# Gathered rows turned later, eight weight subtractions on GpSimd, activation parts ahead of weight parts

## The chip, the core and the metric

The kernel runs on one core of a Trainium2 chip. A core has five engines that each work through a queue of their own in order: TensorE (PE: matrix products and transposes, PEld its weight loads), VectorE (DVE), ScalarE (ACT), GpSimd (POOL) and SyncE (SP, which here issues loads). Sixteen DMA engines move data. The metric is the device time of one execution in microseconds (us), lower is better.

## What is computed

Three stages follow each other. The third, in which the change lies, gives each of 1536 tokens to one of eight experts:

```
attention per (batch, head), where a query sees only keys of its own cluster -> x  (1536 x 512)
x = relu(x @ w_in)**2 @ w_out                                    # 512 -> 2048 -> 512
do = x @ w_skip > 0                                              # the other tokens pass through
e  = argmax(x[do] @ w_gate);  g = softmax(x[do] @ w_gate)[e]
out = x;  out[do] = x[do] + g * (relu(x[do] @ w1[e]) @ w2[e])    # w1: 8 x 512 x 1024, w2: 8 x 1024 x 512
```

All of it is held to float32 accuracy. A float32 product is made of three products of rounded parts: a value is split into a high part (a rounded copy) and a low part (the value minus its high part), and high x high, high x low and low x high are summed.

## The kernel before

The expert stage works in nine *units* of 128 token slots: units 0 and 1 are two blocks of the fullest expert, units 2 to 8 are the other seven experts. For a unit u the steps are these.

- `gather(u)` (L1013): GpSimd issues an indirect DMA that brings the unit's rows into a tile (`u`, or `l` for every third). Its list of rows comes from the routing: `ixA` for unit 0, `ixB` for unit 1, `ixp` for the rest. Unit 0 gathers from `out_dram`, the others from `xd`, a copy of the same rows.
- `parts(src, name)` (L1021): four transposes on TensorE into a PSUM tile `xps`, of which there are two in turn, shared with the routing's transposes at L819. Then ScalarE writes the high part (L1028: `xh` for gathered rows, `hh` for the hidden layer), and VectorE the low part (L1029: `xl`, `hl`).
- `g1(u, n)` (L1039): one half n of the hidden layer, 12 products with `wih`, `wil` into `hps`, and a Relu on ScalarE (L1043) into `hs`. `turn_h(u, n)` is `parts` of `hs`. `g2(u, n)` (L1049): 12 products with `woh`, `wol` into `acc`. `finish(u)` (L1054): VectorE scales and adds, GpSimd issues an indirect write of the rows to `out_dram`.

Expert weights are loaded by SP in pieces of 128 x 1024 into stage buffers (`st`, and `xc`, the tiles of the earlier stages). `half_weights` (L746) splits each piece: ScalarE writes the high part (L761), VectorE the low part in two subtractions of 128 x 512 (L765). The tables `ENG0`, `ENG1`, `ENG2` name the two engines for each piece of the first, the second and the later experts; each entry is `'av'` before: ScalarE and VectorE. A stage buffer is free for the next load when both have read it. The second expert's pieces are needed from unit 2 on.

Up to the beginning of unit 1 a hand-written order stands: `base()` (L1129) yields once per three products (last products of the middle stage, then unit 0), and `EVENTS` says at which count n other work is called: `'c'` a weight piece, `'l'` a step of the routing of the last 384 tokens (`late()`, L986), `'x'` `parts` of unit 0's gathered rows. A routing step `turn_x` (L812) also writes its rows to `xd` and `out_dram` from ScalarE's queue (L815, L816), transposes them (L819) and copies them out of PSUM (`xs`, L821); the logits (L825) read `xs`. Later `late()` computes ranks and a payload (`pay`, L896), sums them on TensorE (`sl`, L919), makes `ixB` and calls `gather(1)`.

`between(gen, f)` calls f after two of a generator's four groups of three products. From unit 1 on the loop at L1179 sets the order. In this stage TensorE's queue keeps the order in which the code is written (and SP's too, up to unit 1); ScalarE, VectorE and GpSimd are ordered by a scheduler that goes by priority (the order of the code) and by what it thinks is ready.

Of the kernel before, what the change touches and what calls it, by code (L numbers as in the profile page):

```python
# [7 lines left out]
F32 = mybir.dt.float32  # L8
# [4 lines left out]
ALU = mybir.AluOpType  # L13
# [23 lines left out]
PE, ACT, DVE, POOL, SP = (mybir.EngineType.PE, mybir.EngineType.Activation, mybir.EngineType.DVE,  # L37
                          mybir.EngineType.Pool, mybir.EngineType.SP)
EVENTS = ((1, 'e'), (2, 'e'), (3, 'e'), (4, 'e'), (8, 'e'), (11, 'e'), (12, 'c'), (13, 'e'), (15, 'c'),
          (16, 'cce'), (18, 'el'), (21, 'x'), (22, 'lcc'), (25, 'c'), (26, 'l'), (28, 'lc'), (30, 'l'), (34, 'll'))  # L40
ENG0 = ('av',) * 8
ENG1 = ('av',) * 8
ENG2 = ('av',) * 8
HOLD = 2
M0 = {DVE, PE, ACT, POOL}
AFTER = 0
PACE = 3
# [5 lines left out]
def clustered_attention_moe(  # L53
# [16 lines left out]
    nc = tc.nc  # L70
# [29 lines left out]
    inner = ExitStack()  # L100
    inner.enter_context(tc.manual_schedule(engines=M0))
    nc.vector.memset(slot, 1.0)
# [30 lines left out]
    def do(gen):  # L133
        for _ in gen:
            pass
# [130 lines left out]
    with ExitStack() as actx:  # L266
# [417 lines left out]
        for i in range(-LA, NQ + GT + 1):  # L684
            if i == CLOSE:
                inner.close()
            for op in ORDER.split():
                op, lag = op.rstrip("'"), op.count("'")
# [38 lines left out]
    loads = [h + (c,) for h in halves for c in (0, 2)]  # L727
    ENGS = [ENG0, ENG1] + [ENG2] * E

# [5 lines left out]
    def stage(t):  # L735
        free.append(t[:, 0:1024].rearrange("p (c f) -> p c f", c=2))
# [47 lines left out]
    def econvert_to(units):  # L784
        while edone[0] < min(units, len(halves)):
            if next(egen) == "unit":
                edone[0] += 1
# [173 lines left out]
    def early():  # L961

        for ch in range(NC - 1):
# [8 lines left out]
            if ch == NC - 2:  # L972
                pick(0, sg)
                gather(0)
            if ch < HOLD:
                stage(xc[ch])
# [9 lines left out]
    def late():  # L986
# [5 lines left out]
        gather(1)  # L992
        for ch in range(HOLD, NC):
            stage(xc[ch])
# [14 lines left out]
    UN = E + 1  # L1009
# [3 lines left out]
    def gather(u):  # L1013

        xg = xgs[u % 3]
        nc.gpsimd.memset(xg, 0.0)
        nc.gpsimd.indirect_dma_start(
            out=xg, in_=xd if u else out, in_offset=bass.IndirectOffsetOnAxis(ap=lists[u][0], axis=0),
            out_offset=None, bounds_check=N - 1, oob_is_err=False)

    def parts(src, name):  # L1021

        tps = ps_x.tile([128, 4, 128], F32, name="xps", tag="x")
        for c in range(4):
            nc.tensor.transpose(out=tps[:, c], in_=src[:, c * 128:(c + 1) * 128], identity=ident)
        hh = ep.tile([128, 4, 128], F32R, name=name + "h")
        hl = ep.tile([128, 4, 128], F32R, name=name + "l")
        nc.scalar.copy(out=hh, in_=tps)  # L1028
        nc.vector.tensor_tensor(out=hl, in0=tps, in1=hh.bitcast(F32), op=ALU.subtract)  # L1029
        return hh, hl  # L1030

    def products(ps, x, w, start, stop):
        for c in range(4):
            for i, (a, b) in enumerate(((0, 0), (0, 1), (1, 0))):
                nc.tensor.matmul(out=ps, lhsT=x[a][:, c], rhs=w[b][:, c],
                                 start=(start and c == 0 and i == 0), stop=(stop and c == 3 and i == 2))
            yield

    def g1(u, n):  # L1039
        hps = ps_h.tile([128, 512], F32, name="hps")  # L1040
        yield from products(hps, xp_t[u], hexp[max(u - 1, 0), 0, n], True, True)
        hs = ep.tile([128, 512], F32, name="hs")
        nc.scalar.activation(out=hs, in_=hps, func=AF.Relu)  # L1043
        hs_t[u, n] = hs

    def turn_h(u, n):
        hp_t[u, n] = parts(hs_t.pop((u, n)), "h")

    def g2(u, n):  # L1049
        if n == 0:  # L1050
            y_t[u] = ps_o.tile([128, DM], F32, name="acc")
        yield from products(y_t[u], hp_t.pop((u, n)), hexp[max(u - 1, 0), 1, n], n == 0, n == FB - 1)

    def finish(u):  # L1054
        yo = ep.tile([128, DM], F32, name="yo", bufs=1)
        nc.vector.scalar_tensor_tensor(out=yo, in0=y_t.pop(u), scalar=lists[u][1], in1=xgs[u % 3],
                                       op0=ALU.mult, op1=ALU.add)
        nc.gpsimd.indirect_dma_start(  # L1058
            out=out, out_offset=bass.IndirectOffsetOnAxis(ap=lists[u][0], axis=0),
            in_=yo, in_offset=None, bounds_check=N - 1, oob_is_err=False)  # L1060
# [82 lines left out]
    def between(gen, f):  # L1143
        for i, _ in enumerate(gen):
            if i == 1:
                f()
            yield

    def x_of_A():
        xp_t[0] = parts(xgs[0], "x")  # L1150
# [25 lines left out]

    econvert_to(6)
    xp_t[1] = parts(xgs[1], "x")
    for u in range(1, UN):  # L1179
        econvert_to(4 * u)  # L1180
        do(g1(u, 0))
        if u > 1:
            do(g2(u - 1, 1))
            finish(u - 1)
            turn_h(u, 0)
        if u + 2 < UN:
            gather(u + 2)
        econvert_to(4 * u + 2)
        do(g1(u, 1) if u > 1 else between(g1(u, 1), lambda: turn_h(u, 0)))
        if u + 1 < UN:  # L1190
            xp_t[u + 1] = parts(xgs[(u + 1) % 3], "x")
        do(g2(u, 0))
        turn_h(u, 1)
    do(g2(UN - 1, 1))
    finish(UN - 1)

# [65 lines left out]
```

## Time and profile before

| | |
|---|---|
| time of three runs, us | 686.8, 688.0, 688.48 (median 688.0) |
| the profiled execution, us | 688.21, of which the span is 686.5 |
| busy over the span, us | PE 655.3 (95%), DVE 481.0 (70%), ACT 415.1 (60%), POOL 253.0 (37%) |
| instructions | PE 3769, DVE 928, ACT 846, POOL 329 |

The span is what the trace covers; the time has 1.7 us around it. Times in the rows are microseconds from the span's start. The routing of the last tokens and units 0 and 1 lie between about 540 and 590, units 2 to 8 between about 586 and 678, and the last write follows. In a timeline row the bracket gives how long the engine was idle ahead of the instruction and what ended the wait. Matmul durations overlap: the spacing of starts is what counts.

### The profile page before, as it was taken

The page shows a single profiled execution, that of the slowest core. Times are in us where ns is not written, and L with a number is a line of the kernel's source. Part 1 is how long each engine was busy: PE and PEld are TensorE (multiplying, and loading weights), DVE is VectorE, ACT ScalarE, POOL GpSimd, SP SyncE. Part 2 cuts the span into 40 slices and gives each one's busy share as a digit, 9 for nine tenths or more (in the row PEclk, how much of TensorE's full clock was granted, in tenths as well). Part 3 has the DMA queues.
Part 4 walks back from the last instruction along what each step waited for, and adds up shares of the span by engine and source line. Part 5 has one row for each costly group of instructions (what it writes and reads, how often), then busy time and mean ns, then how long its engine had stood idle before and what let it go on. Part 6 is the DMA issues. An engine that isn't in the chain of part 4 may idle for free. (4 is left out here: it accounts for less than half of the span.)

```text
span 686.5 us, 11273 instructions
## 1 busy us (share of the span) xinstructions
PE 655.3 (95%) x3769; PEld 569.2 (83%) x3769; DVE 481.0 (70%) x928; ACT 415.1 (60%) x846; POOL 253.0 (37%) x329
## 2 busy tenths in 40 slices
PE   7889999999999999899999999999999898999994
PEld 6688988988888888889899999999888676888883
DVE  5678999999999999664365656522244688899950
ACT  6779989989998986444433333322232275778830
POOL 4534555536365445644344453421110203113110
PEclk9999999999999999999999999999999989999998
DMA  6567565655655200213212222101222596999900
GB/s 138 144 163 198 136 160 134 149 139 137 149 122 126 55 13 1 69 62 103 67 63 77 69 71 91 40 0 47 93 91 82 177 336 243 369 361 362 364 14 23
DMA packets 72034, 89.90 MB, mean 131 GB/s; under 512 B 32384, under 2 KB 43584, under 8 KB 71968
## 3 DMA queue, kind: packets, MB, share of 16 engines
q1 hardware_dynamic: 69664, 84.52, 41.7%
q0 software_dynamic: 1440, 3.01, 1.2%
q10 hardware_dynamic: 864, 1.57, 0.6%
q8 instruction: 32, 0.52, 0.3%
q14 instruction: 34, 0.28, 0.1%
HBM read 62.18 MB, written 9.44 MB: 104 GB/s over the span
## 5 line engine op out<-in xcount | busy, mean ns | idle before, releaser
L580 DVE TENSOR_TENSOR pl<-pt,ph 128x384 fp32r<-128x384 f32 x192 | 103.5, 550 | 19.8 <-ACT ph L571 18.3
L259 ACT ACTIVATE r<-hps 128x384 f32<-128x384 f32 x62 | 30.4, 491 | 125.8 <-PE hps L252 120.6
L557 PE MATMUL pt<-ident,p 128*128 128x128 f32 x576 | 97.1, 279 | 4.7 <-DVE pl L580 3.7
L515 PE MATMUL sc<-B,A 80*128 80x384 f32 (+1 forms) x384 | 93.4, 364 | 4.5 <-DMA A<-hi 1.8
L571 ACT CAST ph<-pt 128x384 fp32r<-128x384 f32 x192 | 89.7, 480 | 10.5 <-PE pt L557 9.7
L522 DVE TENSOR_REDUCE nm<-sc 128x1 f32<-128x768 f32 x96 | 90.9, 947 | 3.5 <-PE sc L515 3.4
L262 DVE TENSOR_TENSOR hl<-r,hh 128x384 fp32r<-128x384 f32 x62 | 37.4, 604 | 77.0 <-POOL hh L138 77.0
L531 ACT ACTIVATE p<-sc,nm 128x768 f32<-128x768 f32 x96 | 87.3, 909 | 6.0 <-DVE nm L522 5.5
L557 PEld LDWEIGHTS pt<-ident,p 128*128 128x128 f32 x576 | 70.8, 142 | 20.2 <-DVE pl L580 13.1
L138 POOL TENSOR_SCALAR hh<-r 128x384 fp32r<-128x384 f32 x62 | 36.5, 589 | 137.9 <-ACT r L260 118.8
L1087 PE MATMUL acc<-woh,hh 128*128 128x512 f32 x186 | 74.6, 401 | 0.0
L1087 PE MATMUL acc<-woh,hl 128*128 128x512 f32 x186 | 73.9, 397 | 0.0
L1087 PE MATMUL acc<-wol,hh 128*128 128x512 f32 x186 | 73.9, 397 | 0.0
L590 PE MATMUL av<-ph,vs 128*128 128x384 f32 x192 | 73.4, 382 | 0.1
L515 PEld LDWEIGHTS sc<-B,A 80*128 80x128 f32 (+1 forms) x384 | 63.9, 193 | 9.6 <-ACT p L531 5.3
L590 PE MATMUL av<-pl,vs 128*128 128x384 f32 x192 | 65.7, 342 | 0.6 <-DVE pl L580 0.6
L252 PE MATMUL hps<-A,wil 128*128 128x384 f32 x184 | 62.1, 338 | 1.8 <-POOL wil L184 1.8
L252 PE MATMUL hps<-A,wih 128*128 128x384 f32 x184 | 62.5, 340 | 0.0
L252 PE MATMUL hps<-B,wih 128*128 128x384 f32 x184 | 62.1, 337 | 0.0
L1087 PEld LDWEIGHTS acc<-woh,hl 128*128 128x128 f32 x186 | 35.3, 190 | 8.0
L1087 PEld LDWEIGHTS acc<-woh,hh 128*128 128x128 f32 x186 | 35.2, 190 | 5.8 <-DVE xc L1095 0.2
L1087 PEld LDWEIGHTS acc<-wol,hh 128*128 128x128 f32 x186 | 35.3, 190 | 5.3
(260 smaller groups left out, 1474.6 us busy)
## 6 DMA issues: line engine op xcount, KB each, us to landing
xc<-in_moe_w_dram SPq DMA_DIRECT2D x34, 512.0 KB, 5.8
st<-in_moe_w_dram SPq DMA_DIRECT2D x30, 512.0 KB, 5.7
st<-in_moe_w_in_dram SPq DMA_DIRECT2D x64, 128.0 KB, 2.9
st<-in_moe_w_out_dram SPq DMA_DIRECT2D x16, 512.0 KB, 3.5
A<-hi SPq DMA_DIRECT2D x30, 192.0 KB, 3.1
B<-hi SPq DMA_DIRECT2D x30, 192.0 KB, 3.1
qn<-in_q_dram SPq DMA_DIRECT2D x16, 192.0 KB, 3.3
kn<-in_k_dram SPq DMA_DIRECT2D x16, 192.0 KB, 3.6
```

The lines of the kernel that those rows point to most:

```text
L138: nc.gpsimd.tensor_scalar(out=o, in0=i, scalar1=1.0, scalar2=0.0, op0=ALU.mult, op1=ALU.add)
L252: nc.tensor.matmul(out=hps, lhsT=wi[w][:, c, f * 128:(f + 1) * 128], rhs=xhl[ch][a][:, c], start=(n == 0), stop=(n == 3 * KD - 1))
L259: nc.scalar.activation(out=r, in_=hps, func=AF.Relu)
L262: nc.vector.tensor_tensor(out=hl, in0=r, in1=hh.bitcast(F32), op=ALU.subtract)
L515: nc.tensor.matmul(out=sc[:, c, 0:384], lhsT=A[h][0:kk, a, t * 128:(t + 1) * 128], rhs=Bk[h][0:kk, a, c * 384:(c + 1) * 384], start=(a == ...
L522: nc.vector.tensor_reduce(out=nm_t[i], in_=sc_t[i][:, :, 0:384], op=ALU.max, axis=AX.XY, negate=True)
L531: nc.scalar.activation(out=p, in_=sc[:, :, 0:384], func=AF.Exp, bias=nm, scale=1.0, accum_out=su_t[n, c][:, t, h:h + 1])
L557: nc.tensor.transpose(out=pt[:, c], in_=p_t[i][:, n, c * 128:(c + 1) * 128], identity=ident)
L571: nc.scalar.copy(out=block(i, n)[by_pool].bitcast(F32) if by_pool else block(i, n)[0], in_=pt_t[i, n])
L580: nc.vector.tensor_tensor(out=pl, in0=pt_t.pop((i, n)), in1=ph.bitcast(F32), op=ALU.subtract)
L590: nc.tensor.matmul(out=av, lhsT=vs[:, c, 2 * h:2 * h + 2].rearrange("p x d -> p (x d)"), rhs=r[:, c], start=(c == 0 and i == 0), stop=(c = ...
L1087: nc.tensor.matmul(out=acc, lhsT=h2[a][:, i * 128:(i + 1) * 128], rhs=wo[w][:, f], start=(f == 0 and n == 0), stop=(f == NF - 1 and n == 2))
```

## The change

Four edits, all in the expert stage.

1. The event `'x'` (transposes and parts of unit 0's gathered rows) moves from count 21 to count 24, so three groups of three products later.
2. `ENG1` gets `'ap'` in its first four entries: the low parts of the second expert's `w1`, eight subtractions of 128 x 512, are made by GpSimd instead of VectorE.
3. In `parts` the two part instructions are traced at a priority raised by 120, so that the scheduler may set them ahead of weight parts.
4. In the last unit the transposes of the second hidden half stand inside the products `g2(u, 0)`, after two of their four groups, instead of behind them.

```
-          (16, 'cce'), (18, 'el'), (21, 'x'), (22, 'lcc'), (25, 'c'), ...
+          (16, 'cce'), (18, 'el'), (22, 'lcc'), (24, 'x'), (25, 'c'), ...
-ENG1 = ('av',) * 8
+ENG1 = ('ap',) * 4 + ('av',) * 4
+AHEAD = 120
@@ parts
-        nc.scalar.copy(out=hh, in_=tps)
-        nc.vector.tensor_tensor(out=hl, in0=tps, in1=hh.bitcast(F32), op=ALU.subtract)
+        with tc.high_priority(offset=AHEAD):
+            nc.scalar.copy(out=hh, in_=tps)
+            nc.vector.tensor_tensor(out=hl, in0=tps, in1=hh.bitcast(F32), op=ALU.subtract)
@@ for u in range(1, UN)
-        do(g2(u, 0))
-        turn_h(u, 1)
+        if u + 1 < UN:
+            do(g2(u, 0))
+            turn_h(u, 1)
+        else:
+            do(between(g2(u, 0), lambda: turn_h(u, 1)))
```

**GpSimd, from unit 0's gather on.** `wil` is the low part of `w1`; the rows with `ixA`, `ixB` and `ixp` are the gathers of unit 0, 1 and 2. Before:

```order
L1017 DMA u<-out_dram,ixA 128x512
L1017 DMA u<-xd,ixB 128x512
L1017 DMA l_5821<-xd,ixp 128x512
L1058 DMA out_dram<-yo,ixA 1536x512
L1016 MEMSET u 128x512
```

After:

```order
L1018 DMA u<-out_dram,ixA 128x512
L766 TENSOR_TENSOR wil<-xc_91,wih 128x512 x2
L766 TENSOR_TENSOR wil<-xc_92,wih 128x512 x2
L766 TENSOR_TENSOR wil<-st,wih 128x512 x4
L1018 DMA u<-xd,ixB 128x512
L1018 DMA l_5821<-xd,ixp 128x512
L1060 DMA out_dram<-yo,ixA 1536x512
```

The eight subtractions stand between the gather of unit 0 and that of unit 1, in GpSimd's one queue.

**TensorE, around unit 0's gathered rows.** `acc` are the last products of the middle stage, `xps<-ident,u` the transposes of the gathered rows, `xps<-ident,xc_94` those of a routing block, `lps` the logits of the block before it, `hps` the first products of unit 0. Before (the row after the last one here is the first `hps`):

```order
L1025 MATMUL xps<-ident,u 128x128 x4
L1087 MATMUL acc<-woh,hh 128x512
L1087 MATMUL acc<-wol,hh 128x512
L1087 MATMUL acc<-woh,hl 128x512
L819 MATMUL xps<-ident,xc_94 128x128 x4
L825 MATMUL lps<-wgs,xs 128x9 x4
L1087 MATMUL acc<-woh,hh 128x512
L1087 MATMUL acc<-wol,hh 128x512
L1087 MATMUL acc<-woh,hl 128x512
```

After (the three products ahead of the first row have moved up):

```order
L820 MATMUL xps<-ident,xc_94 128x128 x4
L826 MATMUL lps<-wgs,xs 128x9 x4
L1089 MATMUL acc<-woh,hh 128x512
L1089 MATMUL acc<-wol,hh 128x512
L1089 MATMUL acc<-woh,hl 128x512
L1089 MATMUL acc<-woh,hh 128x512
L1089 MATMUL acc<-wol,hh 128x512
L1089 MATMUL acc<-woh,hl 128x512
L1026 MATMUL xps<-ident,u 128x128 x4
L1037 MATMUL hps<-wih,xh 128x512
L1037 MATMUL hps<-wil,xh 128x512
```

The transposes of the gathered rows stood nine products, a routing block and its logits ahead of the first `hps`; now they stand right ahead of it.

**ScalarE, at the same place.** `DMA xd` and `DMA out_dram` are a routing block's writes, `COPY xs` its copy, `CAST xh` the gathered rows' high part. Before:

```order
L815 DMA xd<-xc_94 128x512
L761 CAST wih<-st 128x1024
L816 DMA out_dram<-xc_94 128x512
L761 CAST wih<-st 128x1024
L821 COPY xs<-xps 128x512
L761 CAST wih<-st 128x1024
L1028 CAST xh<-xps 128x512
L761 CAST wih<-xc_91 128x1024
```

After:

```order
L816 DMA xd<-xc_94 128x512
L762 CAST wih<-st 128x1024
L817 DMA out_dram<-xc_94 128x512
L762 CAST wih<-st 128x1024
L822 COPY xs<-xps 128x512
L762 CAST wih<-st 128x1024
L816 DMA xd<-xc_94 128x512
L762 CAST wih<-xc_91 128x1024
L1030 CAST xh<-xps 128x512
```

Up to the first `COPY xs` the rows are the same; `CAST xh` stands one weight cast and one write later.

## Rows read from the trace of the kernel before

**Rows 1.** Stretches of 20 us: busy time (x instructions), granted clock, DMA share, GB/s.

```profile
540.00:560.00 20.00, 17.20 (x85) 13.65 (x84) 13.21 (x24) 10.08 (x13) 1.56 (x1) 0.83 0.95 333
560.00:580.00 20.00, 17.00 (x81) 12.88 (x81) 17.81 (x58) 11.46 (x15) 6.63 (x5) 0.91 0.73 243
600.00:620.00 20.00, 20.00 (x96) 16.39 (x95) 19.53 (x33) 15.47 (x21) 3.92 (x4) 1.00 1.02 362
```

**Rows 2.** Timeline of TensorE, unit 0's gathered rows: start, duration, instruction, [idle before].

```profile
548.19 0.66 PE L1025 MATMUL xps<-ident,u 128*128 128x128 f32 x4 [2.61 <-DMA u<-out_dram,ixA]
...
551.08 1.71 PE L825 MATMUL lps<-wgs,xs 128*128 128x9 f32 x8
...
553.21 0.63 PE L1087 MATMUL acc<-wol,hh 128*128 128x512 f32 x1
...
555.35 0.58 PE L1035 MATMUL hps<-wih,xh 128*128 128x512 f32 x1
```

**Rows 3.** Timeline of ScalarE: the write that waits, what stands behind it, later casts.

```profile
548.17 0.37 ACTq L816 DMA_DIRECT2D out_dram<-xc  x1
548.59 1.05 ACT L761 CAST wih<-st 128x1024 fp32r<-128x1024 f32 x1 [4.51 <-DMA u<-out_dram,ixA]
549.54 0.58 ACT L821 COPY xs<-xps 128x512 f32<-128x512 f32 x1
...
561.40 1.03 ACT L761 CAST wih<-xc 128x1024 fp32r<-128x1024 f32 x1
```

**Rows 4.** Timeline of GpSimd: the gathers of unit 0 and of unit 1.

```profile
540.58 1.56 POOL L1017 DMA_INDIRECT u<-out_dram,ixA  x1 [0.62 <-DVE hl L262]
570.09 1.38 POOL L1017 DMA_INDIRECT u<-xd,ixB  x1 [27.95 <-DMA xc<-in_moe_w_dram]
```

**Rows 5.** Instructions that write `wil`: ns min/median/max, first and last start.

```profile
L765 DVE TENSOR_TENSOR wil<-st,wih x30: 674/682/694, 544.1 to 652.0; 128x512 fp32r<-128x512 f32 x30
L184 POOL TENSOR_TENSOR wil<-u,wih x16: 1277/1390/1715, 102.1 to 436.4; 128x512 fp32r<-128x512 f32 x16
```

**Rows 6.** DMA issues from 535 to 600: queue, count, median us from issue to landing.

```profile
u<-out_dram,ixA POOLq DMA_INDIRECT x1, 7.6
u<-xd,ixB POOLq DMA_INDIRECT x1, 3.6
l<-xd,ixp POOLq DMA_INDIRECT x1, 4.8
```

**Rows 7.** Timeline of TensorE: the payload's wait, then unit 1's gathered rows.

```profile
568.03 0.24 PE L919 MATMUL sl<-pay,so 128*128 128x40 bf16 x3 [1.10 <-DVE pay L896]
...
574.62 0.60 PE L1025 MATMUL xps<-ident,u 128*128 128x128 f32 x4
575.89 0.50 PE L1035 MATMUL hps<-wih,xh 128*128 128x512 f32 x1 [0.67 <-ACT xh L1028]
...
576.82 0.50 PE L1035 MATMUL hps<-wih,xl 128*128 128x512 f32 x1 [0.20 <-DVE xl L1029]
```

**Rows 8.** Timeline of VectorE: a moved subtraction, the payload, unit 1's list.

```profile
562.96 0.69 DVE L765 TENSOR_TENSOR wil<-xc,wih 128x512 fp32r<-128x512 f32 x1
...
567.70 0.27 DVE L896 TENSOR_TENSOR pay<-oh,vals 128x120 bf16<-128x120 bf16 x1
...
569.66 0.15 DVE L929 SCALAR_TENSOR_TENSOR ixB<-sB 128x1 int32<-128x1 f32 x1
```

**Rows 9.** Timeline of the last unit: its `g2` halves and the transposes between.

```profile
670.47 0.39 PE L1035 MATMUL acc<-woh,hh 128*128 128x512 f32 x1
...
670.73 0.60 ACT L1043 ACTIVATE hs<-hps 128x512 f32<-128x512 f32 x1 [2.28 <-PE hps L1035]
...
673.27 0.60 PE L1025 MATMUL xps<-ident,hs 128*128 128x128 f32 x4
...
674.54 0.51 PE L1035 MATMUL acc<-woh,hh 128*128 128x512 f32 x1 [0.68 <-ACT hh L1028]
...
675.27 0.50 PE L1035 MATMUL acc<-woh,hl 128*128 128x512 f32 x1
```

More of the change, by code (lines that the diff above doesn't have):

```diff
@@ L39 @@
 EVENTS = ((1, 'e'), (2, 'e'), (3, 'e'), (4, 'e'), (8, 'e'), (11, 'e'), (12, 'c'), (13, 'e'), (15, 'c'),
-          (16, 'cce'), (18, 'el'), (21, 'x'), (22, 'lcc'), (25, 'c'), (26, 'l'), (28, 'lc'), (30, 'l'), (34, 'll'))
+          (16, 'cce'), (18, 'el'), (22, 'lcc'), (24, 'x'), (25, 'c'), (26, 'l'), (28, 'lc'), (30, 'l'), (34, 'll'))
 ENG0 = ('av',) * 8
-ENG1 = ('av',) * 8
+ENG1 = ('ap',) * 4 + ('av',) * 4
 ENG2 = ('av',) * 8
 HOLD = 2
+AHEAD = 120
 M0 = {DVE, PE, ACT, POOL}
```

## The prediction

> **What bounds the kernel now.** I read the busy time by stretches first, then TensorE's timeline where it is not full, then the queues of whoever it waits for. [...]
>
> At unit 0's gathered rows it idles 2.61 us, and ScalarE is stuck at the same point: its write to `out_dram` (548.17) goes only when the gather, which reads `out_dram`, has landed (540.58 + 7.6 = 548.2), and behind that write stand a cast and the copy `xs`, done at 549.54 + 0.58 = 550.12 [rows 2 to 4, 6]. Around the routing of the last tokens it waits 1.10 us for the payload, then 0.67 and 0.20 us for unit 1's parts [rows 7]. In the last unit it waits 0.68 us for `hh`, and a little more for `hl` [rows 9].
>
> [...] Products start every 0.233 us at the upper level (12 in 2.80 us) [rows 9] and every 0.43 us at the lower (553.21 to 555.35, five products) [rows 2].
>
> **Edit 1, gathered rows three groups later.** TensorE goes on where it stood: three products (0.7 us) and a routing block's transposes (0.6 us), from 545.6 to 546.9. Next in its queue are the logits, which need `xs`. In ScalarE's order nothing ahead of that copy has moved, so it still ends at 550.12. The idle spell is then about 3.2 us instead of 2.6 us. The logits start at about 550.1 instead of 551.08, a gain of 1.0 us; owed are the gathered rows' transposes (0.4 us at the upper level, 0.9 us at the lower). And those now stand right ahead of the first `hps`, so that `xh` and `xl`, hidden before by some 6 us of other work, are waited for. The same sequence exists for unit 1: 0.67 + 0.20 us of waiting [rows 7]. Sum: -1.0 + 0.4 to 0.9 + 0.9, so 0.3 to 0.8 us later, and I take 0.6. [...]
>
> **Edit 2, eight subtractions to GpSimd.** What it removes: VectorE's eight subtractions of 0.68 us [rows 5], of which the first stands at 562.96, inside the chain of small routing operations that ends in the payload at 567.70 [rows 8]. Four of the eight lie ahead of the payload, 2.4 us and more; TensorE's wait of 1.10 us for it goes, even with unit 0 shifted by 0.6. [...] TensorE is then ready for unit 1's gathered rows not at 574.62 but at 574.62 + 0.6 - 1.1 = 574.1, or 572.3 if the clock stays up.
>
> What it adds: GpSimd takes 1.28 to 1.72 us for this shape, median 1.39 [rows 5], and the order of after puts all eight between the gathers of unit 0 and unit 1, in one queue. The first can start when ScalarE's cast of the first piece of that expert is done: 561.40 + 1.03 = 562.4 before [rows 3], 563.2 with the shift of edit 1 and its knock-on on ScalarE. Eight of them take 10.2 us (minimum) to 11.1 us (median), so the queue is free at 573.4 to 574.3; I take 573.9. The gather of unit 1 went out at 570.09 before, as soon as its list was ready at 569.66 + 0.15 [rows 4, 8]. Now the list waits for the queue, and the gather leaves 3.8 us later.
>
> It has little slack to pay this from. It took 3.6 us to land (573.7), 0.9 us ahead of the transposes that read it [rows 6, 7]. For a gather that leaves at 573.9 the nearest row is the next one, 4.8 us, issued as weight loads picked up again; the ends are 3.6 and, among busy loads, 7.6 us [rows 6]. So it lands at 578.7, with 577.0 and 581.5 as ends. Behind this wait on TensorE stands all the rest, since unit 1's first products need those rows. Against 574.62 that is **+4.1 us** (+2.4 to +6.9). Edit 1's shift and the saved payload wait are both swallowed by it.
>
> [...] By the two rows of the clock this costs 1.8 to 3.4 us [rows 1]; the first part of it passes in the wait for `xh` and `xl`, so I take the lower end, **+1.8 us**.
>
> VectorE still makes the low parts of `w2` pieces at this time, from two inputs in SBUF. The median and the maximum of GpSimd's row differ by 0.33 us [rows 5], which eight times is 2.7 us. [...] I stay with the median, since it was taken with VectorE at work too (70% of the span).
>
> **Edit 3, parts ahead of weights.** In units 2 to 8 there is no wait of TensorE to remove [rows 1], so nothing is gained. The price is that ScalarE and VectorE now stand at a part that waits for TensorE while a weight piece could be done. Cover: VectorE's last `wil` starts at 652.0 [rows 5], while the last unit's first half of `hps` begins 36 products ahead of 670.47 [rows 9], at about 662, so pieces are some 9 us early. I cost it at zero; without that cover it would be up to one part, 0.6 to 0.7 us, per unit.
>
> **Edit 4, last transposes inside products.** `hs` is ready at 670.73 + 0.60 = 671.3; six products after 670.47 is 671.9, so the transposes need not wait. The two parts then pass under the other six products. The wait of 0.68 us goes, and of 675.27 - 674.54 = 0.73 us between the first and third product 0.47 remains: 0.68 + 0.27 = 0.95, so **-1.0 us**. Nothing later covers this; it counts in full.
>
> **Sum.** +4.1 + 1.8 - 1.0 = +4.9 us. The profiled execution took 688.21 us, 0.2 us more than the median of 688.0, so I add the sum to the median: 692.9 us. With the ends of the gather and of the clock: +2.4 + 0 - 1.0 = +1.4 gives 689.4, +6.9 + 3.4 - 1.0 = +9.3 gives 697.3.
>
> **Rivals.** *The cast comes early.* If the clock holds at unit 0, ScalarE's cast of the second expert's first piece comes some 2 us earlier (560.4), the queue is free at 571.5, and the gather, with still idle DMA engines, lands at 575.1. That is +0.5 for the gather, -1.0 for the tail, 0 to +1.8 for the clock: 687.5 to 689.3, no change. [...]
>
> *Faster: the relief of VectorE decides.* If the queue on GpSimd let the gather go by about 568.7, it would land when TensorE is ready at 572.3. Then the payload's 1.1 us, the second fall of the clock, 1.8 us, and the tail's 1.0 us are won, less the 0.6 of edit 1: 684.7. It takes eight subtractions in some 5.5 us, 0.69 us each, VectorE's own pace; GpSimd's shortest row is 1.28 us. It decides from the point where GpSimd is done before unit 1's list is.
>
> *Much slower: contention and loads.* With 1.72 us each [rows 5] the queue is free at 576.9, the loads run again, the gather takes 7.6 us [rows 6] and lands at 584.5: +9.9 + 3.4 - 1.0 = +12.3, 700.3 us.
>
> **How the numbers follow.** A measurement of this kernel can tell about 0.3% (2.1 us) from no change. Forecast 0.60 (in 689.4 to 697.3, of which the lowest 0.02 lies within 0.3%), the early cast 0.21, the faster rival 0.09, much slower 0.10. Faster by over 0.3%: 0.09. Within: 0.21 + 0.02 = 0.23. Slower: 0.58 + 0.10 = 0.68. The range reaches from 687.3, which takes in the early cast, to 697.3; what is left out is the faster rival and the much slower one.
>
> **What the profile of after would show.** Edit 1: idle of about 3 us ahead of the logits, released by ScalarE's `xs`, not by the gather; a wait for `xh` ahead of unit 0's first product. Edit 2: eight `wil` subtractions on GpSimd of 1.3 to 1.4 us from about 563 to 574, the gather of unit 1 right behind them, some 4 us of TensorE idle ahead of `xps<-ident,u` with that gather as releaser, and a lower clock after it; no wait for the payload. Edit 4: no wait ahead of the last `acc` products. Were the gather to leave before 571, or TensorE not to wait for it, the forecast would be wrong and the time near or below that of before.

## The result, and the profile after

The changed kernel takes 694.32 us (median of 6 runs, 693.73 to 696.52) where the kernel before took 687.95 us beside it (6 runs, 686.8 to 688.97): a ratio of 1.010, with a 95% interval of 1.0081 to 1.0119. The forecast was 692.9 us, slower, with a range of 687.3 to 697.3. The sign, the rough size and the edit that costs were forecast; the mechanism was not the one named, as the rows show.

The profiled execution took 696.52 us, with a span of 694.8 us, 8.3 us more than the one before. Line numbers are one or two higher than before. Stretches of 20 us, columns as in [rows 1]:

```profile
540.00:560.00 20.00, 15.86 (x76) 12.25 (x76) 11.50 (x25) 8.10 (x11) 2.07 (x2) 0.83 0.88 301
560.00:580.00 20.00, 13.39 (x64) 10.74 (x64) 19.46 (x53) 11.15 (x15) 11.83 (x10) 0.85 0.59 208
580.00:600.00 20.00, 19.32 (x91) 15.28 (x91) 14.67 (x24) 11.32 (x15) 4.27 (x4) 0.98 0.83 295
```

Between 560 and 580 TensorE is busy 13.39 us where it was 17.00, and VectorE, though eight subtractions lighter, 19.46 us where it was 17.81. Work was taken from VectorE and it became busier, which already speaks against the forecast. The timeline of TensorE, with the rows that answer to [rows 2, 7]:

```profile
550.95 1.88 PE L826 MATMUL lps<-wgs,xs 128*128 128x9 f32 x8 [3.47 <-ACT xs L822]
555.39 1.05 PE L1026 MATMUL xps<-ident,u 128*128 128x128 f32 x4
557.12 0.50 PE L1037 MATMUL hps<-wih,xh 128*128 128x512 f32 x1 [0.68 <-ACT xh L1030]
...
567.09 0.17 PE L874 MATMUL rk<-oh,tri 128*128 128x24 bf16 x1 [2.58 <-DVE oh L870]
...
575.91 0.24 PE L920 MATMUL sl<-pay,so 128*128 128x40 bf16 x3 [3.71 <-DVE pay L897]
...
582.37 0.60 PE L1026 MATMUL xps<-ident,u 128*128 128x128 f32 x4
```

At unit 0 the picture is the one forecast: ScalarE's write stands until the gather has landed, and `xs` behind it, as in [rows 3]:

```profile
548.95 0.37 ACTq L817 DMA_DIRECT2D out_dram<-xc  x1
549.37 1.04 ACT L762 CAST wih<-st 128x1024 fp32r<-128x1024 f32 x1 [4.55 <-DMA u<-out_dram,ixA]
...
550.32 0.58 ACT L822 COPY xs<-xps 128x512 f32<-128x512 f32 x1
```

The wait for the payload, forecast to go, has grown from 1.10 to 3.71 us, and the one ahead of the ranks (`rk`, which reads `oh`), 0.47 us in the trace of before, to 2.58 us. Ahead of unit 1's gathered rows at 582.37, where the forecast put the stall, there is no wait. GpSimd's timeline, answering to [rows 4]:

```profile
541.33 1.56 POOL L1018 DMA_INDIRECT u<-out_dram,ixA  x1 [0.62 <-DVE hl L263]
564.51 4.98 POOL L766 TENSOR_TENSOR wil<-xc,wih 128x512 fp32r<-128x512 f32 x4 [21.62 <-PE xps L1026]
569.45 5.33 POOL L766 TENSOR_TENSOR wil<-st,wih 128x512 fp32r<-128x512 f32 x4
578.13 1.40 POOL L1018 DMA_INDIRECT u<-xd,ixB  x1 [3.36 <-DVE sgp L999]
```

The eight subtractions end at 569.45 + 5.33 = 574.8, and then GpSimd sits idle for 3.36 us until unit 1's list is there: the queue waits for the list, not the list for the queue. The rows land after 3.5 us, as in [rows 6], at 581.6, ahead of the transposes at 582.37. Why the list is late, VectorE's timeline tells, answering to [rows 8]:

```profile
564.55 1.26 DVE L867 TENSOR_TENSOR oh<-oh,mr 128x24 f32<-128x24 f32 x1
565.74 0.16 DVE L889 TENSOR_REDUCE gate<-ex 128x3 f32<-128x24 f32 x1
565.85 1.19 DVE L870 TENSOR_TENSOR oh<-oh,sel 128x24 bf16<-128x24 f32 x1
566.96 1.31 DVE L890 TENSOR_SCALAR gate<-gate 128x3 f32<-128x3 f32 x1
...
568.54 0.68 DVE L1031 TENSOR_TENSOR hl<-xps,hh 128x512 fp32r<-128x512 f32 x1
...
569.43 1.33 DVE L909 TENSOR_SCALAR rkb<-rank,nA 128x3 f32<-128x3 f32 x1
570.68 1.34 DVE L895 TENSOR_TENSOR gate<-gate,vals 128x3 f32<-128x3 f32 x1
571.94 1.69 DVE L912 TENSOR_TENSOR so<-slot,rkb 128x384 bf16<-128x384 f32 x1
573.56 1.25 DVE L893 CAST vals<-gate 128x3 bf16<-128x3 f32 x1
...
575.58 0.28 DVE L897 TENSOR_TENSOR pay<-oh,vals 128x120 bf16<-128x120 bf16 x1
577.71 0.15 DVE L930 SCALAR_TENSOR_TENSOR ixB<-sB 128x1 int32<-128x1 f32 x1
```

Operations on 128 x 3 and 128 x 24 elements now last 1.19 to 1.34 us. Two of them in the kernel before:

```profile
562.57 0.18 DVE L866 TENSOR_TENSOR oh<-oh,mr 128x24 f32<-128x24 f32 x1
565.82 0.22 DVE L908 TENSOR_SCALAR rkb<-rank,nA 128x3 f32<-128x3 f32 x1
```

The instructions that write `wil` on GpSimd (ns min/median/max), answering to [rows 5], with two pieces of four subtractions:

```profile
L766 POOL TENSOR_TENSOR wil<-xc,wih x4: 1264/1279/1291, 564.5 to 568.2; 128x512 fp32r<-128x512 f32 x4
L766 POOL TENSOR_TENSOR wil<-st,wih x4: 1269/1300/1602, 569.4 to 573.2; 128x512 fp32r<-128x512 f32 x4
```

A held operation ends with the GpSimd instruction that was running: `oh` 564.55 + 1.26 = 565.81, while GpSimd's first subtraction runs from 564.51 for some 1.26 us (to about 565.8); `rkb` ends at 570.76, GpSimd's fifth, from 569.45, at about 570.75. The seven lengthened rows shown above come to 9.4 us; before they took 1.6 us (0.18 + 0.18 + 0.16 + 0.22 + 0.16 + 0.55 + 0.16). That is 7.8 us more on the chain from the logits to the payload, against the 2.7 us of VectorE's own four subtractions that left it. From VectorE's first operation on the last logits (L858, now L859) to the payload it took 567.70 - 560.63 = 7.07 us and takes 575.58 - 562.60 = 12.98 us.

The last unit, answering to [rows 9], and the write of its rows, before (L1056) and after (L1058):

```profile
677.25 0.39 PE L1037 MATMUL acc<-woh,hh 128*128 128x512 f32 x1
678.64 0.60 PE L1026 MATMUL xps<-ident,hs 128*128 128x128 f32 x4
679.00 0.48 PE L1037 MATMUL acc<-woh,hh 128*128 128x512 f32 x1
...
683.48 0.75 DVE L1058 SCALAR_TENSOR_TENSOR yo<-acc,gp,l 128x512 f32<-128x512 f32 x1 [2.90 <-PE acc L1037]
```

```profile
677.90 0.75 DVE L1056 SCALAR_TENSOR_TENSOR yo<-acc,gp,l 128x512 f32<-128x512 f32 x1 [2.69 <-PE acc L1035]
```

No wait stands there now. From the first product of the last `g2` to the scaling it takes 6.23 us instead of 677.90 - 670.47 = 7.43 us.

One loss lies behind the last product. After all units comes a loop for experts that overflow (L1216, not entered with these inputs); it splits weights by the same table `ENG1`. GpSimd's queue at that line, before (L1211) and after: the semaphore message behind its last write (issued at 678.93 before and 684.51 after, landed 2.9 us later in both), and its three branches, the last of which ends the kernel's work there.

```profile
L1211 POOLq COMPARE_BRANCH  x3: 33/38/45, 679.3 to 684.0; - x3
L1211 POOLq INC_SWDGE_SEM  x1: 539/539/539, 681.9 to 681.9; - x1
```

```profile
L1216 POOLq COMPARE_BRANCH  x3: 41/43/50, 684.9 to 692.3; - x3
L1216 POOLq INC_SWDGE_SEM  x1: 539/539/539, 687.7 to 687.7; - x1
```

From the message to the last branch it was 684.0 - 681.9 = 2.1 us and is 692.3 - 687.7 = 4.6 us: **2.5 us** more. By the code, GpSimd's part of the loop held no weight subtraction before and holds 64 after, eight for each of eight experts, though none runs.

The 8.3 us of this execution, place by place:

| stretch | before | after | difference |
|---|---|---|---|
| start to unit 0's gather (nothing changed there) | 540.58 | 541.33 | +0.75 |
| from there to unit 0's first `hps` (edit 1) | 14.77 | 15.79 | +1.02 |
| to unit 1's transposes (edit 2, mostly) | 19.27 | 25.25 | +5.98 |
| to the last `g2` | 95.85 | 94.88 | -0.97 |
| to the scaling of the last rows (edit 4) | 7.43 | 6.23 | -1.20 |
| to the end of the span (the jump) | 8.60 | 11.32 | +2.72 |

The +5.98 is not edit 2's alone. In the trace of `e_no_pool`, which lacks only edit 2, that stretch takes 20.87 us; by these single traces edit 2 adds 25.25 - 20.87 = 4.38 us beside the other three edits (24.64 - 19.27 = 5.37 us alone, in `e_pool_only`). Of the -0.97, 0.65 lies in unit 2 (12.45 us from its transposes to unit 3's, where it was 13.10); in the fourteen traces here that unit takes 12.45 to 14.55 us.

### The profile page after: what moved, and what is told of

Read it like the earlier page. It is cut to its first block, busy times and chain, and to the rows that moved or that the text cites. A ratio compares the mean times of both kernels' runs of the same rounds, so it can differ in the third digit from the quotient of the medians.

```text
span 694.8 us, 11281 instructions
## 1 busy us (share of the span) xinstructions
PE 654.5 (94%) x3769; PEld 568.8 (82%) x3769; DVE 483.8 (70%) x920; ACT 415.1 (60%) x846; POOL 263.3 (38%) x337
## 3 DMA queue, kind: packets, MB, share of 16 engines
q0 software_dynamic: 1440, 3.01, 1.2%
## 5 line engine op out<-in xcount | busy, mean ns | idle before, releaser
L169 ACT ACTIVATE u<-st 128x512 f32<-128x512 f32 x32 | 21.6, 675 | 31.0 <-DMA st<-in_moe_w_in_dram 25.0
```

## The experiments

Two explanations of edit 2 stood against each other. **Theory 1**: while GpSimd subtracts, VectorE's routing operations are held, so the list is late. **Theory 2**, the prediction's: the list waits in GpSimd's queue behind the subtractions. Times beside the kernel before are ratios with 95% intervals.

**`e_no_pool`: the changed kernel without edit 2.**

```
-ENG1 = ('ap',) * 4 + ('av',) * 4
+ENG1 = ('av',) * 8
```

> The changed kernel with the eight subtractions back on VectorE; its other three edits stay. [...] Theory 3 (the loss is edit 1's new wait for xs and xh) expects 692 us or more.

689.1 us, 1.0003 [0.9987, 1.0019]. By Theories 1 and 2 the loss had to go with edit 2, and it does: edits 1, 3 and 4 together change nothing that can be measured; the loss is edit 2's. They do change the place. TensorE waits 2.22 us for the payload, as in `e_prio_only` (edit 3 alone), where it was 1.10 before: with edit 3 VectorE's `hl` stands ahead of the payload and waits for ScalarE's `hh`. In `e_prio_only`:

```profile
569.67 0.69 DVE L1031 TENSOR_TENSOR hl<-xps,hh 128x512 fp32r<-128x512 f32 x1 [1.20 <-ACT hh L1030]
```

**`e_pool_half`: only four of the eight subtractions on GpSimd.**

```
-ENG1 = ('ap',) * 4 + ('av',) * 4
+ENG1 = ('ap',) * 2 + ('av',) * 6
```

> The changed kernel with only the first four of the eight subtractions on GpSimd; the other four are on VectorE. GpSimd is then done at about 569.5 in the times of the changed kernel, ahead of unit 1's list even as it was before (569.8). Theory 2 (queue) expects no loss against the version with none on GpSimd: 687 to 689 us. Theory 1 (VectorE held up) expects the first three long operations of the chain to stay long (1.26, 1.19 and 1.31 us instead of 0.18, 0.18 and 0.16, so +3.2 us) and the later ones short: 690 to 692 us.

693.29 us, 1.0076 [1.0052, 1.0101]. GpSimd:

```profile
562.91 4.98 POOL L766 TENSOR_TENSOR wil<-xc,wih 128x512 fp32r<-128x512 f32 x4 [22.11 <-PE xps L1026]
573.44 1.40 POOL L1018 DMA_INDIRECT u<-xd,ixB  x1 [5.55 <-DVE sgp L999]
```

The queue is free at 567.9, 5.55 us ahead of the list, and the time is still lost. Theory 2 falls. VectorE's operations beside the four subtractions are held as in the changed kernel:

```profile
562.96 1.26 DVE L867 TENSOR_TENSOR oh<-oh,mr 128x24 f32<-128x24 f32 x1
564.25 1.19 DVE L870 TENSOR_TENSOR oh<-oh,sel 128x24 bf16<-128x24 f32 x1
566.63 1.29 DVE L893 CAST vals<-gate 128x3 bf16<-128x3 f32 x1
```

The time lies above Theory 1's 690 to 692 too, and it is no price of the holding: of the 5.6 us between the spans of this trace and of `e_no_pool` (691.2 and 685.6), 2.3 lie behind the last unit (the loop here holds 32 subtractions), 2.1 in unit 2 (14.55 us, with a wait of 1.45 us for `hh`), and only 0.6 between unit 0's first `hps` and unit 1's transposes.

**`e_pool_w2`: the eight subtractions of the second expert's `w2` on GpSimd instead.** They come later, while unit 1's and unit 2's lists are made.

```
-ENG1 = ('ap',) * 4 + ('av',) * 4
+ENG1 = ('av',) * 4 + ('ap',) * 4
```

> The changed kernel with eight other subtractions on GpSimd: those of the second expert's w2 instead of its w1. Four of them stand ahead of unit 1's gather in GpSimd's queue, but they start only at about 570 to 571, when the payload is done. Theory 2 (queue) expects the gather to leave some 4.5 us late, with the lower clock 692 to 694 us. Theory 1 (VectorE held up) expects the chain up to the payload to be untouched and at most one or two operations behind it to be long: 687 to 690 us.

699.86 us, 1.0184 [1.0135, 1.0234], more than either theory had said. Unit 1's gather leaves at 575.55, 4.4 us later than in `e_no_pool`, and TensorE waits 4.71 us for it; the list, held too, and GpSimd's queue are ready at the same time (575.3), so this run does not separate the theories. VectorE is then held twice for two subtractions on end, and the second time `xl` of unit 1 stands behind it and TensorE waits for that:

```profile
576.70 2.80 DVE L930 SCALAR_TENSOR_TENSOR ixp<-sgp 128x8 int32<-128x8 f32 x1
580.50 2.86 DVE L1213 TENSOR_SCALAR rem<-rem 128x8 f32<-128x8 f32 x1
```

```profile
584.94 0.80 PE L1037 MATMUL hps<-wih,xl 128*128 128x512 f32 x1 [2.66 <-DVE xl L1031]
```

**`e_hi_pool`: GpSimd makes the four high parts (casts of 128 x 1024, one input) and VectorE the subtractions.**

```
-ENG1 = ('ap',) * 4 + ('av',) * 4
+ENG1 = ('pv',) * 4 + ('av',) * 4
```

> The changed kernel with the high parts of the same four pieces on GpSimd (four casts of 128 x 1024 with one input, instead of ScalarE) and the eight subtractions on VectorE. If any GpSimd instruction on SBUF holds up VectorE's two-input and small operations, the chain shows single operations of a microsecond and the time is 690 to 693 us. If only GpSimd instructions with two inputs do that, the operations stay at 0.2 us and the time is 687 to 690 us.

694.48 us, 1.0091 [1.0057, 1.0125], above the 690 to 693 of the reading that came true; the jump takes 689.2 - 684.6 = 4.6 us here as well. GpSimd's casts last 1.04 to 1.27 us and hold VectorE as well, though less often; a subtraction at 567.43 takes 1.27 instead of 0.68 us, a cast of three columns 0.92:

```profile
567.43 1.27 DVE L766 TENSOR_TENSOR wil<-xc,wih 128x512 fp32r<-128x512 f32 x1
568.71 0.92 DVE L893 CAST vals<-gate 128x3 bf16<-128x3 f32 x1
```

The order on VectorE differs too (a weight part and `hl` stand ahead of `oh`), so how much is the holding and how much the order is not separated here.

**`e_pool_third`: the same eight subtractions, but the third expert's**, which run in unit 1, when no routing is left.

```
-ENG1 = ('ap',) * 4 + ('av',) * 4
+ENG1 = ('av',) * 8
-    ENGS = [ENG0, ENG1] + [ENG2] * E
+    ENGS = [ENG0, ENG1, ('ap',) * 4 + ('av',) * 4] + [ENG2] * E
```

> The changed kernel with the GpSimd subtractions moved by one expert: those of the third expert's w1 go to GpSimd, those of the second stay on VectorE. By then the routing chain is over. Theory 1 (VectorE's routing operations are held up) expects no cost there, since TensorE has weights in hand: 687 to 690 us, as with none on GpSimd. If eight subtractions on GpSimd cost by themselves, through their own time or later weights, 692 us or more.

688.7 us, 1.0011 [0.9995, 1.0026]: no cost that can be measured. The two engines still hold each other; six subtractions take 1.5 us each on GpSimd, three take 1.54 us each on VectorE, but TensorE waits for none of them:

```profile
585.58 9.00 POOL L766 TENSOR_TENSOR wil<-st,wih 128x512 fp32r<-128x512 f32 x6
```

```profile
590.49 4.63 DVE L766 TENSOR_TENSOR wol<-xc,woh 128x512 fp32r<-128x512 f32 x3
```

The run also isolates the jump at the end. It executes as many subtractions on GpSimd as the changed kernel, but the loop behind the units uses `ENG1` and holds none:

```profile
L1216 POOLq COMPARE_BRANCH  x3: 33/38/45, 679.4 to 684.1; - x3
L1216 POOLq INC_SWDGE_SEM  x1: 539/539/539, 682.0 to 682.0; - x1
```

684.1 - 682.0 = 2.1 us, as before.

**`e_pool_only`: the kernel before with edit 2 alone.**

```
-ENG1 = ('av',) * 8
+ENG1 = ('ap',) * 4 + ('av',) * 4
```

> The kernel before with edit 2 alone, the eight subtractions on GpSimd. If VectorE's small routing operations are held up by GpSimd's subtractions, the loss is all here and nothing of it hangs on edits 1, 3 and 4: 693 to 696 against 688, TensorE idle 2 to 4 us ahead of the ranks or the sums, the list of unit 1 about 7 us later than in the kernel before. If instead the three edits together made the loss (the later gathered rows leave VectorE's chain more exposed), 688 to 690.

695.8 us, 1.0118 [1.0078, 1.0158]. TensorE waits 2.56 us for the ranks and 5.22 us for the payload; the jump is there as well, 690.0 - 685.5 = 4.5 us. In the traces of the five kernels with a GpSimd entry in `ENG1`, 9.8 to 10.3 us pass from the issue of the last write to the end of the span; in the nine others it is 7.5 to 8.2 us. From the message to the last branch it is 4.4 to 4.6 us with 64 subtractions in the loop, 4.2 us with 32 (`e_pool_half`), 4.6 us with 32 casts (`e_hi_pool`), and 2.1 us in all nine others: the loss is there with half the number, too, and does not grow in proportion.

**`e_x_only`: edit 1 alone.**

```
-          ... (18, 'el'), (21, 'x'), (22, 'lcc'), (25, 'c'), ...
+          ... (18, 'el'), (22, 'lcc'), (24, 'x'), (25, 'c'), ...
```

> The kernel before with edit 1 alone, the gathered rows turned three products later. By the prediction's step 0.3 to 0.8 us later: a wait of TensorE of about 3.2 us ahead of the logits for the copy xs, in place of 2.6 us ahead of the transposes for the gather, and about 0.7 us ahead of the first hps for xh. The rival is a gain of 1.0 us or more, should the clock stay up or xh be ready in time.

695.03 us, 1.0100 [1.0066, 1.0134], a miss by both readings. The wait for `xs` is there (3.01 us), and so is that for `xh` (0.68 us), but `xl` stands behind six weight subtractions on VectorE:

```profile
559.36 0.68 DVE L1029 TENSOR_TENSOR xl<-xps,xh 128x512 fp32r<-128x512 f32 x1
```

```profile
560.09 0.79 PE L1035 MATMUL hps<-wih,xl 128*128 128x512 f32 x1 [2.24 <-DVE xl L1029]
```

Before, other products lay between the transposes and the first `hps`, and `xl` could come late. The logits and the routing chain behind are late in turn, with the granted clock at 0.75 over 540 to 560 (0.83 before): the list `ixB` is written at 578.03 instead of 569.66. In `e_no_pool`, which has edits 1, 3 and 4, `xl` stands right behind `xh` and the loss is not there. Edit 4 acts only in the last unit, so it is edit 3 that makes edit 1 bearable; edits 1 and 3 were not run as a pair.

**`e_prio_only`: edit 3 alone.**

```
+        with tc.high_priority(offset=AHEAD):
             nc.scalar.copy(out=hh, in_=tps)
             nc.vector.tensor_tensor(out=hl, in0=tps, in1=hh.bitcast(F32), op=ALU.subtract)
```

> The kernel before with edit 3 alone, the parts traced ahead of the weight pieces. By the prediction's step no change, 688.0 to 689.0, and no gap of TensorE in units 2 to 8; the rival is a cost of 0.6 to 0.7 us per unit where a weight piece comes late, 692 or more.

689.94 us, 1.0020 [1.0001, 1.0039]: no change by the bound of 0.3%, but above the 688.0 to 689.0 expected, and the interval leaves out 1. The 2.22 us for the payload shown above, and 2.11 us for `hs` ahead of unit 0's second transposes, are the places where its trace waits longer.

**`e_tail_only`: edit 4 alone.**

```
-        do(g2(u, 0))
-        turn_h(u, 1)
+        ... the same for u + 1 < UN, else:
+            do(between(g2(u, 0), lambda: turn_h(u, 1)))
```

> The kernel before with edit 4 alone, the last transposes inside the products. By the prediction's step 1.0 us earlier: 687.0 to 687.9 against 688.2 to 688.6, a ratio of about 0.9985, with no wait ahead of the last products. The rival, that the two parts now compete with the scaling of the output, gives no change.

687.35 us, 0.9981 [0.9963, 1.0000], 1.3 us less, as expected within the interval. From the first product of the last `g2` to the scaling it takes 6.24 us, as within 0.01 us in every kernel here with edit 4, and 7.43 or 7.44 us in those without.

Three runs sought a better kernel. **`e_fix`**: edits 1, 3 and 4, with the write to `out_dram` issued behind the copy `xs`, so that ScalarE is not stuck ahead of it.

```
-        q.dma_start(out=outv[T // TT, T % TT], in_=x1[T])     (ahead of the transposes)
+        q.dma_start(out=outv[T // TT, T % TT], in_=x1[T])     (behind the copy xs)
```

> The changed kernel with no subtractions on GpSimd, and with a routing block's write to out_dram issued behind the copy xs on ScalarE instead of ahead of it. If the idle spell at unit 0 is kept up by that write, which waits for the gather with xs stuck behind it, then xs is done at about 544.6, TensorE goes on without a stop until the gathered rows, which have landed by then, the clock stays up, and unit 0 starts some 5 us earlier: 681 to 685 us. If instead the rows themselves or the weight casts behind the write are what it waits for, the gain is 1 us or less: 687 to 688 us.

687.43 us, 0.9992 [0.9967, 1.0016], so no change, as by the second reading: the wait for `xs` is gone, but the write still holds ScalarE until 549.23, and now `xh` is late: 2.20 us ahead of the first `hps`. What is gained there is lost again: that product starts at 552.17 (554.84 in `e_no_pool`), but TensorE then waits 3.52 us for the payload, and unit 1's transposes start at 575.68 (575.71). In these two traces the routing chain, and not the start of unit 0, sets that time.

**`e_after_list`: the kernel before, with the second expert's subtractions kept behind unit 1's list on VectorE.**

```
+        listed.append(nc.cur_bb.bb.instructions[-1])      (in the routine that makes ixB)
-    econvert_to(6)
+    with tc.issue_after(listed[1]):
+        econvert_to(6)
```

> The kernel before with one thing changed: the eight subtractions stay on VectorE, but queue behind the operation that makes unit 1's list, so none of them stands inside the routing chain and GpSimd does nothing for them. If the eight inside the chain are what holds the payload and the list back, the payload comes 2 us or more earlier, the list about 3 us, TensorE's wait of 1.1 us goes and the second fall of the clock (1.8 us) may go: 684.5 to 687 us where before takes 688. If the chain is held by its own steps, nothing changes: 688 us.

687.81 us, 0.9997 [0.9982, 1.0012]. The wait for the payload is gone, but TensorE reaches the sums only at 567.44, behind its own products and a wait for `hs`, and the list is there at 569.20 instead of 569.66; TensorE then waits 1.25 us for unit 1's gathered rows. Relief of VectorE, the prediction's faster rival, is worth nothing that can be measured here, even where it costs nothing.

**`e_best`: edits 1, 3 and 4, the subtractions behind the list, and the last blocks' `out_dram` writes issued by GpSimd.**

```
+        (q if T < NT - GT else nc.gpsimd).dma_start(out=outv[T // TT, T % TT], in_=x1[T])
+    with tc.issue_after(listed[1]):
+        econvert_to(6)
```

> All that the runs so far point to: edits 1, 3 and 4, no subtractions on GpSimd, the eight on VectorE queued behind unit 1's list, and the last routing blocks' writes to out_dram issued from GpSimd's queue, idle there, so that ScalarE is never stuck behind unit 0's gather. If ScalarE's stuck queue makes the idle spell at unit 0 and the eight subtractions the wait for the payload, unit 0 starts some 4 to 5 us earlier, the clock stays up, unit 1 follows 3 to 6 us earlier, and the tail gives 1 us: 680 to 684 us. If weights or loads bound unit 0, 685 us or more.

686.67 us, 0.9976 [0.9957, 0.9996]: 1.7 us faster than the kernel before, with an interval that ends just below 1, where 4 and more were expected if ScalarE's stuck queue decided; the other reading, 685 us or more, came true. ScalarE no longer waits for the gather, but for weight loads, and `xh` stands behind their casts:

```profile
547.11 1.05 ACT L762 CAST wih<-st 128x1024 fp32r<-128x1024 f32 x1 [2.65 <-DMA st<-in_moe_w_dram]
```

```profile
550.76 0.50 PE L1039 MATMUL hps<-wih,xh 128*128 128x512 f32 x1 [2.35 <-ACT xh L1032]
```

## Why the prediction was right, and where it was not

**What bounds the kernel.** Right for what stands ahead of the last write: that loss lies at the places named, and none of it in units 2 to 8. The jump behind the last unit is at none of them.

**Edit 1 (+0.6 forecast).** Right in place and kind: 3.47 us of idle for `xs` instead of 2.61 for the gather, then 0.68 for `xh`; +1.02 in the trace, a little over the upper end of 0.8. Its own price in the time was not measured, as `e_no_pool` has edits 3 and 4 too. The working left unsaid that it holds only with edit 3.

**Edit 2, what it removes.** Wrong: "TensorE's wait of 1.10 us for it goes". Taking four subtractions of 0.68 us out of VectorE's chain was counted as a gain of 2.4 us; but the chain met GpSimd's instructions of some 1.3 us in their place, and TensorE waits 2.58 + 3.71 us.

**Edit 2, what it adds.** The step that failed is "now the list waits for the queue". GpSimd was done at 574.8, within a microsecond of the 573.9 worked out, but the list came at 578.0, after it. The rows were forecast at 578.7 and landed at 581.6. Unit 1's transposes were forecast 4.1 us later and came 582.37 - 574.62 = 7.75 us later, 7.00 without the 0.75 that stands ahead of the change, which is outside the forecast's +2.4 to +6.9. That the total came near is luck: both mechanisms grow with the same eight instructions of 1.3 us one after the other, and the clock term, counted behind the transposes, lies ahead of them. In `e_pool_half` the two mechanisms part. The prediction's own sign of being wrong, that TensorE would not wait for the gather, did appear; the time that it tied to that sign, near or below that of before, did not.

**GpSimd's pace, and VectorE's.** The prediction weighed only how much longer GpSimd might take, and stayed with its median of 1.39 us; GpSimd ran near its minimum [rows 5], with medians of 1.28 and 1.30 us and one instruction of 1.60, and VectorE paid. In the trace of after, six tensor-tensor, tensor-scalar and cast operations on 128 x 3 and 128 x 24 last 1.19 to 1.34 us beside those instructions, and a tensor-tensor on 128 x 384 lasts 1.69 us where it took 0.55. Two reductions there keep 0.16 and 0.17 us (565.74, 569.13), a reciprocal 0.18 us (568.30), a copy and a tensor-tensor that read PSUM 0.14 and 0.17 us (568.39, 568.45), and `hl`, with one of its two inputs in PSUM, its 0.68 (568.54). What sets the held apart from the others was not shown. GpSimd's instructions stood in one unbroken row, and seven of VectorE's operations each found one of them running.

**The clock (+1.8).** About right in size. That the gather's longer wait would bring it was the author's estimate, and no run shows the term: that wait did not come. In stretches of 1 us the trace of before has a granted clock of 1.00 in the idle spells, of 0.50 from 549 to 555, behind the 2.61 us, and again from 570 to 572, behind the 1.10 us; products start every 0.23 us at 1.00 and every 0.43 us at 0.50. In the trace of after it is 0.50 from 551 to 557, 568 to 570 and 578 to 580, behind waits of 3.47, 2.58 and 3.71 us. The means are 0.83, 0.85 and 0.98 over the three stretches from 540 to 600, against 0.83, 0.91 and (as read in the trace of before) 1.00, so 20 x (0.06 + 0.02) = 1.6 us of full speed more. Wrong in place: the lower level was to meet unit 1's start, but there, from 584.70 on, products start 0.23 us apart. It met unit 0's products behind the waits for the ranks and the payload (0.43 us apart from 567.67 to 570.23 and from 577.58 to 580.57), so it is part of the +5.98 and not a term beside it.

**Edit 3 (0).** Alone within the 0.3% (1.0020), wrong as part of the whole. It was costed in units 2 to 8, and its work is at unit 0, where it spares edit 1 the 6.7 us of `e_x_only`. Its price, VectorE standing at a part that waits, was named for those units alone; it shows ahead of the payload, where TensorE's wait grows from 1.10 to 2.22 us (`e_prio_only`, `e_no_pool`).

**Edit 4 (-1.0).** Right: -1.20 in the trace.

**What was missing.** The 2.5 us of the jump at the end. The diff's table entry reaches code that does not run; the prediction followed `ENG1` only where it is executed.

By medians the sum is 694.32 - 687.95 = 6.4 us against 4.9 forecast; 2.5 us are the jump, so all the rest, with the tail's gain, came to some 3.9 us. The profiled execution lies 2.2 us above its median; 0.75 us of the 8.3 stands ahead of anything the change touches (in the fourteen traces that gather is issued at 539.2 to 541.5); the rest of the difference between the two sums is not assigned.

## What to carry to other kernels

Before work is moved to GpSimd, list what VectorE does at that time: if it is a chain of short operations that somebody waits for, each operation may last as long as one of GpSimd's instructions (here 1.19 to 1.34 us instead of 0.16 to 0.22). The cost is then the number of operations that meet one, times that duration (seven here, 7.8 us more), set against the work saved (2.7 us). The same move cost nothing that could be measured where TensorE did not wait for VectorE (`e_pool_third`). And follow a table's entries through all code that reads it, also through a loop that is not entered: here the jump over it took 2.5 us longer.

## What the runs showed of the hardware

- VectorE's operations of 0.15 to 0.22 us on a few columns lasted 1.19 to 1.34 us beside GpSimd's 128 x 512 subtractions of 1.26 to 1.60 us (medians 1.28 and 1.30), and 2.80 and 2.86 us beside two of them on end (`e_pool_w2`); two reductions (0.16 and 0.17 us) and three operations with an input in PSUM (0.14, 0.17 and, for `hl`, 0.68 us) kept their time (`after`).
- A one-input cast on GpSimd (1.04 to 1.27 us) held VectorE too, up to a subtraction of 1.27 instead of 0.68 us (`e_hi_pool`).
- Where VectorE's own work was large, both lost: 1.5 us each instead of 1.28 on GpSimd, 1.54 instead of 0.68 on VectorE (`e_pool_third`).
- A jump of GpSimd's over a loop body that had grown by 32 or 64 instructions took 2.1 to 2.5 us longer (4.2 to 4.6 us from the last message to the last branch, against 2.1 us in the nine kernels without them). In the trace of after, one transfer of instructions lies between 690 and 692, ahead of the last branch at 692.3; before, the last such transfer lies between 682 and 684, ahead of the branch at 684.0. That fits a loading of code behind the jump, which remains an inference: the trace does not tell which engine a transfer serves.
